# The first 23 microseconds of a fused spectral-mixing and GEGLU backward kernel, put in another order

## The chip, the cores and the metric

The kernel runs on one core of one Trainium2 chip. The metric is the device time in microseconds. Before the change it is 1395.79 us, the median of 4 runs that lie between 1395.49 and 1397.18. One more execution was taken with the hardware profiler on; all durations in this text come from it.

## The reference

The forward function gates two branches row by row. Branch A is a learned filter in the two-dimensional frequency domain, branch B a GEGLU feed-forward block. The kernel computes the output and the gradients with respect to everything but `B_x`, which branch B doesn't use: both branches read the same `x`.

```python
x = A_x                                              # 2048 x 576, bf16
g = sigmoid((x * gate_w).sum(-1, keepdims=True))
a = irfft2(rfft2(x) * (w_r + 1j * w_i))              # over rows and columns
b = (gelu(x @ w_gate) * (x @ w_up)) @ w_down         # F = 4608
out = g * a + (1 - g) * b
_out, vjp = jax.vjp(f, A_x, A_w_r, A_w_i, B_w_gate, B_w_up, B_w_down, gate_w)
grads = vjp(grad_out)                                # grad_out is dO below
```

## The kernel before

**Tiling.** The 2048 rows are 16 tiles of 128 rows; four of them form a row block, so there are four row blocks (`m`). The 4608 hidden columns are 18 groups (`g`) of 256. The outer loop runs over `g`, the inner one over `m`. For each pair the kernel computes `z = dO @ w_down.T` (lines 413 and 418), `xy = x @ [w_gate, w_up]` (lines 422 and 429), the gelu and its derivative on ScalarE and VectorE (lines 441 to 497), and stores the products for later. Between these, TensorE also does the weight gradients of the group before (lines 541, 559, 573) and pieces of the Fourier transforms (lines 602 to 875), which are written as products with sine and cosine tables. A last stage (line 1210) computes the gradient with respect to `x`.

**Layouts.** TensorE contracts over the partition axis, so `x` and `dO` are needed with their 576 columns on the partitions: `xT` and `dOT`, in five chunks of columns (four of 128 and a tail of 64). They are made by TensorE: a product with the identity matrix turns 128 x 128 elements into PSUM (`titems`, lines 378 to 384), and ScalarE or VectorE copies the result out (line 385). One call of `titems` gives three items, with chunks 0 and 1, chunks 2 and 3, and the tail; each item takes one PSUM buffer and one copy. The first group's `w_down` is turned in the same way into `wdT`; for the later groups a DMA transposes.

**PSUM.** While group 0 is computed there are four pools: `pg` with two buffers (transposes, and the small product of the gate), `ph` with two (`xy`, and some transposes as `fx`), and `pz` with one (`z`, and the warm-up). A transpose into `pg` waits until the copy out of the buffer that was used two turns before is done.

**The head.** The order of all work is written out by hand; no scheduler changes it. SyncE issues the loads in the order dO (tiles 0 to 3), `w_down` of group 0, `x` (tiles 0 to 3), the gate and up weights, and then the other tiles of dO and `x` in turn. A load waits for the completion of one about eight loads earlier, since the completion semaphores are reused. ScalarE's queue carries the one-row load of `gate_w` and the weights' tails. TensorE runs 30 products with the identity as warm-up (line 896), turns `gate_w` (line 901), and then turns dO and `w_down`. `H_mm(g, m, between)` computes `z` chunk by chunk and calls the functions in `between` before the tail chunk of `z`. For the first row block this is `opening`, which turns `x`, computes the sines, the parity tables and the first angles of the row transform, and calls `gate(0)`: 20 products with one column (line 394), a sigmoid (line 396), and two small operations that give `1 - g`, by which `z` is scaled (line 441).

**Tables.** `build_D` makes a cosine and a sine table for the transform over the 576 columns and is called for three sets (`D0`, `D2`, `D4`). Each gives functions for the angles (VectorE, lines 136 and 138), for the sines (ScalarE, lines 141 and 142), and for the tails (VectorE, line 152). `build_R` makes the angles of the transform over the rows (VectorE, lines 165 to 172); its sines come much later. ScalarE needs one function table for sines and another for sigmoids, and loads it when the first sigmoid comes.

Of the kernel before, what the change touches and what calls it, by code (L numbers as in the profile page):

```python
# [9 lines left out]
ACT = mybir.ActivationFunctionType  # L10
ALU = mybir.AluOpType
BF16 = mybir.dt.bfloat16
# [32 lines left out]
def eo(c):  # L45

    return slice(256 * (c % 2) + c // 2, 256 * (c % 2) + 256, 2)
# [208 lines left out]
def kernel(  # L256
# [4 lines left out]
    nc = tc.nc  # L261
    LD = nc.sync
# [6 lines left out]
    unit = Unit(ctx.enter_context(tc.tile_pool(name="unit", bufs=NUNIT, side="right")), "unit")  # L269
# [7 lines left out]
    do_v = grad_out[0].rearrange("(p t) d -> p t d", t=T)  # L277
# [19 lines left out]
    wts = {}  # L297
# [26 lines left out]
    def load_x(t0):  # L324
        LD.dma_start(xn[:, t0:t0 + 4, :], x_v[:, t0:t0 + 4, :])

    def load_do(t0):
        LD.dma_start(dB[:, t0:t0 + 4, :], do_v[:, t0:t0 + 4, :])

    ident = res.tile([P, P], BF16, name="ident")  # L330
    make_identity(nc, ident[:])
    gwr = unit([D], name="gwr")
    nc.scalar.dma_start(gwr[0:1, :], gate_w.rearrange("(o d) -> o d", o=1))
    load_do(0)
    wdn = unit([2, D], name="wdn")
    LD.dma_start(wdn[:], B_w_down[0:FG, :].rearrange("(c p) d -> p c d", p=P))
    load_x(0)
    load_w(0, 0, nc.scalar)
    for k in range(1, 4):
# [30 lines left out]
    def titems(src, dst, t0, ps, copies, n=4):  # L370
# [15 lines left out]
            return f  # L386
        return [item(k, cs) for k, cs in enumerate(((0, 1), (2, 3), (4,)))]

    def gate(k):
        lps = pgtile()  # L390
        ts = slice(4 * k, 4 * k + 4)
        for t in range(4 * k, 4 * k + 4):
            for ci in range(5):
                nc.tensor.matmul(lps[:, t:t + 1], lhsT=xT[:, ci, t, :], rhs=gwT[:, (ci, 4 + t % 2)[ci == 4]:][:, 0:1],
                                 start=(ci == 0), stop=(ci == 4))
        nc.scalar.activation(g_bf[:, ts], lps[:, ts], ACT.Sigmoid)
        nc.scalar.activation(omg_bf[:, ts], g_bf[:, ts], ACT.Identity, bias=1.0, scale=-1.0)
        nc.scalar.copy(omg32[:, ts], omg_bf[:, ts])
# [1 line left out]

    kept = {}

    def H_mm(g, m, between=()):

        wgu, wdT = wts[g]
        ts = range(4 * m, 4 * m + 4)
        z = pz.tile([P, 2, 2, FG], F32, tag="z", name="z")

        def zo(t):
            return z[:, t % 2, t % 4 // 2, :]  # L410
        for t in ts:
            for ci in range(4):
                nc.tensor.matmul(zo(t), lhsT=dOT[:, ci, t, :], rhs=wdT[:, ci, :], start=(t % 4 < 2 and ci == 0), stop=False)  # L413
        for f in between:
            f()
        for t in ts:
            r = (LO, HI)[t % 2]
            nc.tensor.matmul(zo(t), lhsT=dOT[r, 4, t, :], rhs=wdT[r, 4, :], start=False, stop=t % 4 >= 2)  # L418
        xy = [ph.tile([P, 2, 2 * FG], F32, tag="xy", name="xy") for _ in range(2)]
        for t in ts:  # L420
            r = (LO, HI)[t % 2]
            nc.tensor.matmul(xy[t % 4 // 2][:, t % 2, :], lhsT=xT[r, 4, t, :], rhs=wgu[r, 4, :], start=True, stop=False)  # L422

        def full(k, between=None):
            for t in ts[2 * k:2 * k + 2]:
                if t % 2 and between:
                    between()
                for ci in range(4):
                    nc.tensor.matmul(xy[k][:, t % 2, :], lhsT=xT[:, ci, t, :], rhs=wgu[:, ci, :], start=False, stop=(ci == 3))  # L429
            return xy[k]  # L430
        return z, full
# [469 lines left out]
        nc.tensor.matmul(gps[r, c:c + 1], lhsT=w, rhs=one[:], start=True, stop=True)  # L901
    D0 = build_D(nc, tb, unit, 0, 2)
    D0[0]()
    D0[1]()
    AC(gwT[:, 0:4], gps[:, 0:4])
    for c, r in ((4, LO), (5, HI)):
        AC(gwT[r, c:c + 1], gps[r, c:c + 1])
    D2 = build_D(nc, tb, unit, 2, 2)
    D2[0]()
    D4 = build_D(nc, tb, unit, 4, 1)  # L910
    parity = iotas_R(nc, tb, res, unit)
    for f in titems(dB, dOT, 0, (pgtile, pgtile, phtile), (VC, AC, VC)):
        f()
    for f in titems(wdn, wts[0][1][:].rearrange("p k (c m) -> p k c m", c=2), 0, (phtile, pgtile, phtile), (AC, VC, VC), n=2):
        f()
    makeB = build_B(nc, tb, unit, res)

    def opening():
        for f in titems(xn, xT, 0, (pgtile, pgtile, pgtile), (VC, AC, VC)):
            f()  # L920
        D2[1]()
        D4[0]()
        D4[1]()
        parity()
        D4[2]()
        build_R(nc, tb, unit, 0)
        gate(0)

    fg = zipped(*fwd_units(xT, scr_x, None)) + zipped(*fwd_units(dOT, scr_g, gs32))
    ia, pa = inv_units(scr_p1, a_dv, SD2)  # L930
# [61 lines left out]
    for g in range(NG):  # L992
# [3 lines left out]
        for m in range(NPR):  # L996
# [15 lines left out]
            if g == 0:  # L1012
                def items(src, dst, t, *cp):
                    return titems(src, dst, 4 * t, (pgtile,) * 3, cp) if t < NPR else [None] * 3
                do1 = items(dB, dOT, 1, VC, VC, VC) if m == 0 else []
                do2 = items(dB, dOT, m + 2, AC, AC, VC)
                x1 = items(xn, xT, m + 1, AC if m else VC, VC, VC)
                z, xy_full = H_mm(g, m, ([opening] if m == 0 else []) + rest)
                rest = []
                da = H_da(g, m, z)  # L1020
                if m == 0:
                    early, mid_, late_ = do1[:2], [do1[2], x1[0]], x1[1:]
                elif m < NPR - 1:
                    early, mid_, late_ = x1[:1], x1[1:], []
                else:
                    early, mid_, late_ = [], [], []
                for f in early:
                    f()
                xy = xy_full(0)
                for f in mid_:  # L1030
                    f()
                if held:
                    held.pop()()
                for part in (1, 0):
                    H_act(0, xy, tiles, part)

                def between():
                    for f in late_:
                        f()
                xy = xy_full(1, between)  # L1040
                for part in range(2):
                    H_act(1, xy, tiles, part)
                if m == 0:
                    build_R(nc, tb, unit, 4)
                    columns_B(nc, tb, res)
                elif m == 1:
                    next(makeB)
                if m < NPR - 1:
                    gate(m + 1)
                else:  # L1050
                    V.tensor_copy(g32[:], g_bf[:])
                    V.tensor_scalar(gs32[:], g32[:], SD2, None, op0=ALU.mult)
                if m + 2 < NPR:
                    do2[0]()
                    rest = do2[1:]
                state += [*H_ew1(g, tiles, da), da]
                held.append(sigs)
            else:
                z, xy_full = H_mm(g, m)
                da = H_da(g, m, z)  # L1060
                for f in inside:
                    f()
                if pr == 5:
                    scale_dB(2, AC)
                xy = xy_full(0)
                if held:
                    scale_dB(0, AC)
                    held.pop()()
                for part in (1, 0):
                    H_act(0, xy, tiles, part)  # L1070
                k0 = int(n > 0 and pr > 7 and ready())
                xy = xy_full(1, fft_next if k0 else None)
                for part in range(2):
                    H_act(1, xy, tiles, part)
                if pr == 5:
                    scale_dB(3, VC)
                state += [*H_ew1(g, tiles, da), da]
                if pr == 4:
                    scale_dB(1, VC)
                elif pr == 5:  # L1080
                    build_R(nc, tb, unit, 8)
                    build_R(nc, tb, unit, 12)
                elif pr == 6:
                    next(makeB)
                side_work(4.4)
                jobs = carry + hs
                total = sum(w for w, _ in jobs)
                at, k = 0.0, k0
                tables = {6: 0}.get(pr)
                for i, (w, f) in enumerate(jobs):  # L1090
                    if k < n and (at >= total * k / n - 0.45 or len(jobs) - i <= n - k):
                        fft_next()
                        k += 1
                    if i == tables:
                        run_late(tb)
                        wcopy[0] = VC
                    if pr == NG * NPR - 1 and at == 0.0:
                        sigs()
                    f()
                    at += w  # L1100
                wcopy[0] = AC
                while k < n:
                    fft_next()
                    k += 1
                flush()
                if pr == 6:
                    next(makeB)
                if pr < NG * NPR - 1:
                    sigs()
# [250 lines left out]
```

## Time and profile before

| what | value |
|---|---|
| median of 4 runs | 1395.79 us |
| the profiled execution | 1397.23 us |
| its span, from the first to the last instruction | 1395.5 us |
| TensorE busy | 1373.7 us, 98% of the span |
| VectorE, ScalarE, GpSimd busy | 740.1, 710.3, 245.4 us |
| granted TensorE clock, mean | 0.999 |
| second row block's `z` starts at | 22.94 us |

In a timeline each row gives the start in microseconds from the start of the span, the time from the start of the first instruction of the row to the end of its last, the engine, the line, the tile written and the tiles read, their shapes, and the number of instructions; idle time before the row and what ended it stand in brackets. PE is TensorE, DVE is VectorE, ACT is ScalarE, POOL is GpSimd and SP is SyncE. Matmuls overlap, so the sum of their durations is longer than the time they take, and a row's end is the end of its last one. In the windows, each engine has its busy time and, in brackets, its number of instructions, in the order PE, weight loads, DVE, ACT, POOL, and then the granted clock (1.00 is full), the busy share of the DMA engines and their rate.

### The profile page before, as it was taken

Reading aid. Unit: us, or ns where it says so; the run is one execution under the profiler, and the core shown is the slowest. Engines: PE = TensorE matmul, PEld = TensorE weight load, DVE = VectorE, ACT = ScalarE, POOL = GpSimd, SP = SyncE. Lnnn points to the kernel's source line nnn. Section 1 sums busy time; section 2 is a strip of 40 time slices with the busy share of each in tenths; the row PEclk is TensorE's granted clock in tenths of the full one; section 3 lists DMA queues with packets and bytes.
Section 4 is the critical chain, followed back from the end, with each engine's and each line's share of the span. In section 5 each row is a group of like instructions: output and inputs, shape, how many; then the busy total and the mean of one; then the engine's idle time right before and its main releaser. Section 6 shows DMA issues by size and latency. Waiting matters only on the chain.

```text
span 1395.5 us, 25930 instructions
## 1 busy us (share of the span) xinstructions
PE 1373.7 (98%) x10186; PEld 913.5 (65%) x10272; DVE 740.1 (53%) x1406; ACT 710.3 (51%) x1311; POOL 245.4 (18%) x486
## 2 busy tenths in 40 slices
PE   8999999999999999999999999999999999999999
PEld 6556566565566556556566566556777777777777
DVE  6975655555889777875666666560001742212101
ACT  6877767777778778767767777661000000000000
POOL 3000111123345634512111101110000100000000
PEclk9999999999999999999999999999999999999999
DMA  6433445355466556555556465749999997777774
GB/s 215 121 92 110 124 111 134 93 144 157 113 163 154 154 146 162 141 145 136 150 140 171 122 169 151 179 110 285 195 192 203 220 194 167 162 157 168 153 153 90
DMA packets 510647, 214.49 MB, mean 154 GB/s; under 512 B 312539, under 2 KB 503709, under 8 KB 510525
## 3 DMA queue, kind: packets, MB, share of 16 engines
q1 hardware_dynamic: 493402, 187.44, 57.2%
q0 software_dynamic: 14912, 24.24, 6.3%
q8 instruction: 80, 1.31, 0.4%
q10 hardware_dynamic: 2210, 1.15, 0.3%
q14 instruction: 43, 0.34, 0.1%
HBM read 41.05 MB, written 93.84 MB: 97 GB/s over the span
## 4 chain that ended last, share of the span: by engine, by line
PE 90%; ACT 2%; issue 1%; DMA 0%; SPq 0%; DVE 0%; ACTq 0%
PE acc L1210 30%; PE wps L559 16%; PE xy L429 15%; PE wps L541 9%; PE z L413 8%; PE wps L573 2%; PE xy L422 2%; PE pf L602 2%; PE z L418 1%; PE pf L619 1%; PE pf L873 1%; PE pf L800 1%; PE pf L711 1%; PE pf L875 1%; ACT ZT L850 0%
## 5 line engine op out<-in xcount | busy, mean ns | idle before, releaser
L1210 PEld LDWEIGHTS <-pin 128*128 128x128 bf16 x3456 | 337.7, 98 | 86.0 <-issue 0.3
L559 PE MATMUL wps<-dH,xn 128*128 128x512 bf16 x1135 | 270.0, 379 | 1.3 <-DVE dwd L510 0.5
L429 PE MATMUL xy<-wgu,xT 128*128 128x512 bf16 x1083 | 259.5, 381 | 8.5 <-issue 7.2
L429 PEld LDWEIGHTS <-xT 128*128 128x128 bf16 x1152 | 106.8, 98 | 134.0 <-issue 26.5
L559 PEld LDWEIGHTS <-xn 128*128 128x128 bf16 x1152 | 111.4, 98 | 118.7 <-issue 1.3
L1227 ACT COPY bo<-acc 128x288 f32<-128x288 f32 x32 | 12.7, 398 | 305.0 <-PE acc L1210 305.0
L541 PE MATMUL wps<-dB,A 128*128 128x288 bf16 x1152 | 154.2, 286 | 0.7 <-DVE dB L990 0.6
L566 POOL DMA_DIRECT2D out_dram<-dw x134 | 72.9, 547 | 432.3 <-ACT dw L510 390.7
L1210 PE MATMUL acc<-wgT,pin 128*128 128x288 bf16 x1152 | 143.8, 286 | 0.0
L1210 PE MATMUL acc<-wuT,pin 128*128 128x288 bf16 x1152 | 143.6, 286 | 0.0
L1210 PE MATMUL acc<-wd_all,pin 128*128 128x288 bf16 x1152 | 142.6, 286 | 0.0
L413 PE MATMUL z<-wdT,dOT 128*128 128x256 bf16 x1152 | 137.5, 273 | 1.3 <-ACT wdT L385 0.8
L541 PEld LDWEIGHTS <-A 128*128 128x128 bf16 x1152 | 112.0, 98 | 34.4 <-issue 1.3
L441 ACT ACTIVATE da<-z,omg 128x256 bf16<-128x256 f32 x288 | 112.1, 472 | 32.9 <-PE z L418 32.9
L413 PEld LDWEIGHTS <-dOT 128*128 128x128 bf16 x1152 | 112.4, 98 | 23.5 <-issue 2.5
L450 ACT CAST xb<-xy 128x512 bf16<-128x512 f32 x144 | 85.4, 593 | 49.9 <-PE xy L429 49.5
L1282 DVE SCALAR_TENSOR_TENSOR f32t<-gwf,dlog,b16t 128x576 f32<-128x576 f32 x16 | 13.1, 817 | 176.0 <-DMA b16t<-dxa_scr 176.0
L448 ACT ACTIVATE q<-xy 128x512 bf16<-128x512 f32 x144 | 88.1, 616 | 7.0 <-PE xy L429 5.0
L451 ACT CAST hu<-xy 128x512 bf16<-128x512 f32 x144 | 87.8, 610 | 0.0
L487 DVE TENSOR_TENSOR xb<-xb,sg 128x1024 bf16<-128x1024 bf16 x48 | 33.2, 691 | 96.5 <-ACT sg L479 96.5
L510 ACT CAST dw<-wps 128x512 bf16<-128x512 f32 x72 | 42.3, 589 | 54.6 <-PE wps L559 52.3
L456 DVE TENSOR_SCALAR s<-q 128x1024 bf16<-128x1024 bf16 x72 | 30.6, 425 | 69.9 <-ACT q L448 69.7
(220 smaller groups left out, 1635.5 us busy)
## 6 DMA issues: line engine op xcount, KB each, us to landing
scr<-dH SPq DMA_DIRECT2D x144, 256.0 KB, 3.4
scr<-A SPq DMA_DIRECT2D x72, 256.0 KB, 2.6
out_dram<-dw POOLq DMA_DIRECT2D x134, 64.0 KB, 2.5
wd_all<-in_B_w_down_dram SPq DMA_DIRECT2D x3, 1728.0 KB, 9.3
out_dram<-dwd POOLq DMA_DIRECT2D x34, 144.0 KB, 2.8
scr_p<-Vt SPq DMA_DIRECT2D x32, 145.0 KB, 3.0
wgu<-in_B_w_gate_dram SPq DMA_DIRECT2D x18, 256.0 KB, 4.2
wgu<-in_B_w_up_dram SPq DMA_DIRECT2D x18, 256.0 KB, 3.4
```

Of the source, the lines that this page charges most:

```text
L413: nc.tensor.matmul(zo(t), lhsT=dOT[:, ci, t, :], rhs=wdT[:, ci, :], start=(t % 4 < 2 and ci == 0), stop=False)
L429: nc.tensor.matmul(xy[k][:, t % 2, :], lhsT=xT[:, ci, t, :], rhs=wgu[:, ci, :], start=False, stop=(ci == 3))
L441: nc.scalar.activation(da[:, t, :], z[:, t % 2, t // 2, :], ACT.Copy, scale=omg32[:, 4 * m + t:4 * m + t + 1])
L448: nc.scalar.activation(q[:, h, :], xy[:, :, 0:FG], ACT.Square)
L450: nc.scalar.copy(xb[:, h, :], xy[:, :, 0:FG])
L451: nc.scalar.copy(hu[:, h, :], xy[:, :, FG:2 * FG])
L487: V.tensor_tensor(xb[:], xb[:], s[:], op=ALU.mult)
L510: wcopy[0](out, in_)
L541: nc.tensor.matmul(wps[:, :288], lhsT=tl(0, t)[:, fch * P:(fch + 1) * P], rhs=dB[:, t, h * 288:(h + 1) * 288], start=(t == 0), stop=(t == ...
L559: nc.tensor.matmul(wps[:].rearrange("p a b -> p (a b)"), lhsT=xn[:, t, c * P:(c + 1) * P], rhs=kt[t // 4][1][:, t % 4].rearrange("p k f -> ...
L566: wst[0].dma_start(ov[:, c, fsl], dw[:, k, :])
L1210: nc.tensor.matmul(acc[:, :288], lhsT=src[:, r, :], rhs=w_of(r)[:, h * 288:(h + 1) * 288], start=(first and r == 0), stop=(last and r == F ...
```

## The change

The change has five parts, all in the head.

1. SyncE loads `w_down` of group 0 before dO, and dO's first four tiles come in two loads of two tiles.
2. `w_down` is turned before dO. VectorE copies its first and last item and ScalarE the middle one. The sines of `D0` follow ScalarE's copy.
3. The first row block's dO is turned by pairs of tiles: `pair` puts all four full chunks of two tiles into one buffer, so that one copy (VectorE for the first pair, ScalarE for the second) completes two tiles. The tail of the four tiles is an item as before.
4. `x` is turned in the middle of `z`: `H_mm` has a new argument `amid`, called after the first two tiles of `z`. `opening` moves there; it turns the tail of `x` first, and VectorE makes all three copies. The gate stays where it was, before the tail of `z`. The first angles of the row transform move behind the first two transposes of the second row block's dO.
5. The sines of `D2` and `D4` are computed before `x` is turned, and after them ScalarE computes a sigmoid of one column that nobody reads, so that the table load comes there and not at the gate.

```diff
-    def load_do(t0):
-        LD.dma_start(dB[:, t0:t0 + 4, :], do_v[:, t0:t0 + 4, :])
+    def load_do(t0, n=4):
+        LD.dma_start(dB[:, t0:t0 + n, :], do_v[:, t0:t0 + n, :])
...
-    load_do(0)
     wdn = unit([2, D], name="wdn")
     LD.dma_start(wdn[:], B_w_down[0:FG, :].rearrange("(c p) d -> p c d", p=P))
+    load_do(0, 2)
+    load_do(2, 2)
     load_x(0)
...
+    def pair(src, dst, t0, ps, cp):
+
+        tp_ = ps(BF16).rearrange("p (c t m) -> p c t m", c=4, t=2)
+        for c in range(4):
+            for tt in range(2):
+                nc.tensor.transpose(tp_[:, c, tt, :], src[:, t0 + tt, eo(c)], ident[:])
+        cp(dst[:, 0:4, t0:t0 + 2, :], tp_)
+
...
-    def H_mm(g, m, between=()):
+    def H_mm(g, m, between=(), amid=None):
...
         for t in ts:
+            if amid and t == ts[2]:
+                amid()
             for ci in range(4):
...
     D0[0]()
-    D0[1]()
     AC(gwT[:, 0:4], gps[:, 0:4])
...
     D4 = build_D(nc, tb, unit, 4, 1)
+    for f in titems(wdn, wts[0][1][:].rearrange("p k (c m) -> p k c m", c=2), 0, (phtile, pgtile, phtile), (VC, AC, VC), n=2):
+        f()
+    D0[1]()
+    pair(dB, dOT, 0, pgtile, VC)
+    pair(dB, dOT, 2, pgtile, AC)
+    titems(dB, dOT, 0, (None, None, phtile), (None, None, VC))[2]()
+    D4[0]()
+    D2[1]()
+    D4[1]()
+    nc.scalar.activation(tb.warm[:], tb.halfpi[:], ACT.Sigmoid)
     parity = iotas_R(nc, tb, res, unit)
-    for f in titems(dB, dOT, 0, (pgtile, pgtile, phtile), (VC, AC, VC)):
-        f()
-    for f in titems(wdn, wts[0][1][:].rearrange("p k (c m) -> p k c m", c=2), 0, (phtile, pgtile, phtile), (AC, VC, VC), n=2):
-        f()
     makeB = build_B(nc, tb, unit, res)
 
     def opening():
-        for f in titems(xn, xT, 0, (pgtile, pgtile, pgtile), (VC, AC, VC)):
+        x0 = titems(xn, xT, 0, (pgtile, pgtile, phtile), (VC, VC, VC))
+        for f in (x0[2], x0[0], x0[1]):
             f()
-        D2[1]()
-        D4[0]()
-        D4[1]()
         parity()
         D4[2]()
-        build_R(nc, tb, unit, 0)
-        gate(0)
...
-                z, xy_full = H_mm(g, m, ([opening] if m == 0 else []) + rest)
+                z, xy_full = H_mm(g, m, [lambda: gate(0)] if m == 0 else rest, opening if m == 0 else None)
...
                 for f in early:
                     f()
+                if m == 0:
+                    build_R(nc, tb, unit, 0)
                 xy = xy_full(0)
```

## The prediction

> **What bounds the kernel now.** I read the page's engine shares first, then TensorE's timeline over the head, then the same stretch in windows (busy time and granted clock), and last ScalarE's and SyncE's timelines.
>
> ```profile
> PE 1373.7 (98%) x10186; PEld 913.5 (65%) x10272; DVE 740.1 (53%) x1406; ACT 710.3 (51%) x1311; POOL 245.4 (18%) x486
> ```
>
> TensorE is the bound over the whole span, and the change touches the first 23 us alone; what it can win is TensorE's idle or slow time there. Its timeline (start, duration, line, what waited):
>
> ```profile
> 5.18 1.07 PE L378 MATMUL pf<-ident,dB 128*128 128x128 bf16 x16
> 6.31 0.39 PE L378 MATMUL fx<-ident,wdn 128*128 128x128 bf16 x4
> 8.11 1.91 PE L413 MATMUL z<-wdT,dOT 128*128 128x256 bf16 x16 [0.82 <-ACT wdT L385]
> 9.86 1.06 PE L378 MATMUL pf<-ident,xn 128*128 128x128 bf16 x16
> 11.25 0.38 PE L384 MATMUL pf<-ident,xn 128*128 128x128 bf16 x4 [0.34 <-DVE xT L385]
> 12.01 0.69 PE L394 MATMUL pf<-gwT,xT 128*128 128x1 bf16 x20 [0.38 <-ACT xT L385]
> 14.98 0.94 PE L378 MATMUL pf<-ident,dB 128*128 128x128 bf16 x8 [0.96 <-ACT g_bf L396]
> 16.57 2.42 PE L429 MATMUL xy<-wgu,xT 128*128 128x512 bf16 x6 [0.22 <-issue]
> 22.94 1.91 PE L413 MATMUL z<-wdT,dOT 128*128 128x256 bf16 x16
> ```
>
> Four waits, 2.5 us by the brackets: on ScalarE's copy of w_down, on the copies of x (two), on the gate. And 16.57: six 512-column products take 2.42, where eight take 1.89 in the next row block (29.24). The windows say why (columns: window, length, busy by engine, clock, DMA share, GB/s):
>
> ```profile
> 8.10:11.60 3.50, 3.15 (x36) 2.76 (x36) 0.69 (x1) 0.65 (x1) 0.00 (x0) 1.00 1.08 360
> 11.60:15.00 3.40, 2.06 (x38) 1.43 (x37) 2.94 (x13) 3.26 (x8) 0.00 (x0) 1.00 1.00 398
> 15.00:18.40 3.40, 3.18 (x14) 1.72 (x15) 2.27 (x6) 1.93 (x6) 0.00 (x0) 0.51 1.02 386
> ```
>
> After a window with 2.06 of 3.40 busy the clock is halved for 3.4 us. ScalarE, which holds two of those waits:
>
> ```profile
> 6.56 1.01 ACT L385 COPY dOT<-pf 128x1024 bf16<-128x1024 bf16 x1
> 7.47 0.59 ACT L385 COPY wdT<-fx 128x512 bf16<-128x512 bf16 x1
> 13.46 1.28 ACT L396 ACT_TABLE_LOAD   x1
> 14.76 0.17 ACT L396 ACTIVATE g_bf<-pf 128x4 bf16<-128x4 f32 x1
> ```
>
> The table load stands in front of the gate's sigmoid, and the second transpose of the next dO waits for the PSUM buffer that this sigmoid reads.
>
> **What the Trainium skill says.** "TensorE: Matmul & The Clock Gate", Part 1: the clock falls to half after a window of about 3.4 us with too little activity, the window runs freely, and so the cold stretch varies between runs. The trace agrees (0.51 for 3.4 us). Part 4 there says that transposes do not count as activity; here the clock stays full after 4.81-8.10, which is nearly all transposes. "ScalarE: Activation LUTs", What ACT_TABLE_LOAD costs: 1283 ns and a drain of 1380; the trace has 1.28 and no drain after it (14.76). "DMA: Bandwidth & Descriptors", Queues, rings and completion order: one queue's descriptors start in ring order, which holds here: dO, w_down and x come in the order issued.
>
> **The change, part by part.** Arithmetic is the same: every transpose, copy and product is still there, one 1-column sigmoid (0.20) is added, and one load is split in two. I restart the head with durations from the rows above and from the same timelines: a 128-column transpose every 0.055 (20 in 5.18-6.3), readable 0.27 after its start (5.57 to 5.84); a z product 0.107; a 512-column product 0.214 (1.67/7 and 1.89/8 less the last one's latency); VectorE copies 0.69, 0.42, 0.28 for 1024, 512, 256 columns; ScalarE copies 1.01 and 0.59.
>
> Loads. SyncE's order becomes w_down (288 KB), two halves of dO (288 KB each), x. Before, dO's 576 KB were the first to land: SyncE's up-projection load, which waits for them, went out at 5.15, and the transposes at 5.18. The first 576 KB now are w_down and half of dO: w_down by 5.1, first half about 5.2-5.8, second at 6.0-6.5 (w_down before: 1.20 + 4.8 = 6.0). The split costs one more issue (0.42), so x is issued at about 2.2 instead of 1.67; the queue ahead of it is busy to 5, so it keeps its place, 1.67 + 6.4 = 8.1. It now waits for the one-row gate load, over by 2.20 when the old gate-weight load with the same wait went out. The gate-weight load now waits for w_down (about 5.1) rather than going at 2.20; the queue ahead (x) is busy to 7, so the transfer starts no later. Later loads wait for earlier ones in the same chain, byte for byte as before. Small tables fall on other buffers, and a few later instructions wait for the gate-row and w_down loads, landed by 6: nothing.
>
> w_down. Transposes at 5.18, 5.40, 5.62, done 5.84. VectorE is free at 5.89 (row 5.43 + 0.46, unchanged): two copies to 6.59. ScalarE: table 5.28, warm-up, three gate copies to 5.87, w_down copy to 6.46, D0 sines (0.86) to 7.3.
>
> dO. The pair copies write four runs of 256 instead of two of 512; no row shows that shape, so 0.69 (as the same columns take) to 1.1 (one column each 1.04 ns); I take 0.69, since the 256-column run in the w_down copy costs no more per column beyond its start. First pair 5.86-6.25, copied by VectorE 6.59-7.27; second pair waits for the w_down buffer (6.46): 6.51-6.9, copied by ScalarE 7.2-8.23; tail to 7.12, copied to 7.81.
>
> z and x. z of the first pair starts at 7.32 (before: 8.11, all of it) and ends 8.18. x tail 8.18-8.40, first half to 8.84, second to 9.28 (ScalarE's buffer free at 8.23). Second z 9.28-10.14, which hides VectorE's copies of x: D4's angles to 8.48, tail to 9.04, 9.74, 10.43. All three on VectorE cost 1.80; without the z between them TensorE would stand 1.1 us. The gate waits for the last, 10.48, ends 11.05.
>
> Sines and table. ScalarE: D2 and D4 sines (0.86 + 0.65) from 8.23 to 9.75, table to 11.04, warm sigmoid 11.24, gate sigmoid at 11.3. The wait of 0.96 is gone, because the table load now runs under x and z. Queued behind it are only g and the da copies, wanted once z ends at 11.28.
>
> Next. z tail and xy tail (0.23 + 0.52) end 11.80; dO of the second row block is needed here, 1.6 us sooner than before. By queue order 2.7 MB lie up to its end; the windows show 0.83 MB moved by 5.0 and 1.75 from 5 to 10, so it lands between 10.9 and 12.2: I charge 0.2. Transposes 12.0-12.88, xy to 14.6, transposes to 15.25. VectorE's R angles (1.14 + 0.43) now stand after these dO copies, at 14.04-15.65, and hold back the next dO and x copies: x buffers at 16.05 and 16.74, where TensorE arrives at 16.1 and 16.54: 0.25 lost. xy ends 17.86, gate and dO transposes 18.94. So the second row block's z starts at about 19.05, against 22.94.
>
> Sum: 22.94 - 19.05 = 3.9 us, of which 2.2 are waits and order and 1.7 the half-clock stretch (eight xy products 15.72-18.82, at full clock 1.71; 3.10 - 1.71 = 1.4, and 0.3 in the transposes before). VectorE and ScalarE move with it: by the same count VectorE's first-block work ends 4.1 sooner, so it does not take the gain back although it is 93% busy from 30 to 65 us. Later stages keep their order.
>
> The profiled execution took 1397.23 for a span of 1395.5: 1397.23 - 3.9 = 1393.3. Its own four timed neighbours run from 1395.49 to 1397.18, median 1395.79; the profiled one is 1.7 above the fastest, the size of one half-clock stretch. From a run without that stretch the gain is 2.2: 1395.49 - 2.2 = 1393.3. Both agree; I take 1393.1, since the 0.2 for dO's landing may not be due.
>
> **Rivals.**
> (1) Everything comes off the median: the 1.4 between profiled time and median is the cost of profiling, and the stretch sits in every run. 1395.79 - 3.9 = 1391.9. For it: the shortage of work at 11.6-15.0 is in the program. Against: two of four timed runs are at 1395.5 and one at 1397.18.
> (2) The half-clock stretch stays, or moves to the first transposes, since the window runs freely. 1393.1 + 1.7 = 1394.8. For: before 4.8 the 30 warm-up products take 3.38, 0.11 each, at half pace. Against: any 3.4 us after 5.2 now hold at least 2.6 of busy time.
> (3) Loads late: the first transfer ramps slowly (165 GB/s mean to 5.0, against 349 after), and w_down comes as 256 rows of 1152 bytes rather than 128 of 4608. If rows, not bytes, set the ramp, w_down is 0.5-1 late, and so is all behind it: 1394.0.
> (4) Slower: the same mechanism at its worst. w_down's wait takes the place of the ScalarE wait, and second-block dO comes late by more than the slack. It decides once w_down lands 2.2 us after 5.18, at 7.4; at 8.0 the time is 1396.1, with the half-clock stretch behind such a hole 1397.8, and past 1398.6 from 8.8 on. Against: w_down landed at 6.0 behind twice its bytes.
> That the change doesn't do what it says: the built order shows the moves, so only the wait could survive it.
>
> **Numbers.** A run cannot tell less than about 0.2% (2.8 us, so below 1393.0 is faster, above 1398.6 slower). Main case 0.58, 1392.2 to 1394.0, half of it under 1393.0; (1) 0.17; (2) 0.11; (3) 0.09; (4) 0.05, of which 0.03 beyond 1398.6. Faster: 0.29 + 0.17 = 0.46; slower 0.03; same 0.51. The range from 1391.6 to 1395.0 takes in (1), (2) and (3).
>
> **What would show it.** TensorE: w_down transposes at 5.2, z in two groups of 8, the first near 7.3, the second near 9.3; no wait on w_down's ScalarE copy; the dO transposes of the second row block without wait on g; second z group of 16 near 19.0; clock 1.00 from 15 to 18.4. ScalarE: table load near 9.8. Wrong if w_down's transposes start after 5.6, if xy of the first row block starts after 13.5, or if row block two gains 3.9 and the end does not.

## The result and the profile after

The changed kernel takes 1393.88 us (median of 42 runs, 1393.44 to 1395.92), the kernel before 1395.61 beside it (60 runs, 1395.46 to 1397.24). The ratio is 0.9987 with a 95% interval of 0.9982 to 0.9991: 1.7 us faster, and within the 0.2% that the prediction calls the same. The time lies in the predicted range (1391.6 to 1395.0), 0.8 above the predicted 1393.1. The profiled execution took 1393.88 for a span of 1392.00, against 1397.23 and 1395.45 before. Nine of the 60 runs of the kernel before lie between 1397.02 and 1397.24, and the execution profiled before is one of that kind: this matters below.

The page's engine shares, after:

```profile
PE 1371.9 (99%) x10186; PEld 913.3 (66%) x10272; DVE 740.7 (53%) x1407; ACT 710.0 (51%) x1311; POOL 244.7 (18%) x486
```

TensorE's timeline over the head, after (columns as in the prediction):

```profile
5.05 0.40 PE L379 MATMUL fx<-ident,wdn 128*128 128x128 bf16 x4
...
7.25 1.05 PE L424 MATMUL z<-wdT,dOT 128*128 128x256 bf16 x8
8.74 0.40 PE L385 MATMUL fx<-ident,xn 128*128 128x128 bf16 x4 [0.44 <-DMA xn<-in_A_x_dram]
...
9.87 1.04 PE L424 MATMUL z<-wdT,dOT 128*128 128x256 bf16 x8
...
12.26 1.07 PE L379 MATMUL pf<-ident,dB 128*128 128x128 bf16 x16
...
19.00 1.25 PE L424 MATMUL z<-wdT,dOT 128*128 128x256 bf16 x10
```

The four waits of before (0.82, 0.34, 0.38, 0.96) are gone. One new one stands there: 0.44 for the transfer of `x`. `w_down` is turned first and in time, `z` comes in two groups of eight, and the second row block's `z` starts at 19.00 instead of 22.94. Two of the stretches shown of before, in windows (length, busy by engine, clock, DMA share, GB/s):

```profile
11.60:15.00 3.40, 3.35 (x34) 2.01 (x33) 2.92 (x9) 2.14 (x7) 0.00 (x0) 1.00 1.03 411
15.00:18.40 3.40, 3.40 (x47) 2.42 (x45) 3.03 (x9) 1.82 (x4) 0.00 (x0) 1.00 1.04 390
```

The thin window (2.06 busy of 3.40) is full now (3.35), and the next one is at full clock. ScalarE's timeline, after:

```profile
9.31 1.28 ACT L930 ACT_TABLE_LOAD   x1
...
11.61 0.17 ACT L405 ACTIVATE g_bf<-pf 128x4 bf16<-128x4 f32 x1 [0.80 <-PE pf L403]
```

The table load runs under `x`'s transposes and the second group of `z`, and the gate's sigmoid now waits for TensorE instead of TensorE for it.

So the head gained what the prediction said, 3.94 us between the two profiles. The time gained less. Where the rest went is seen by following the gain through the program, with the starts of three events in both profiles:

| event | before | after | gain |
|---|---|---|---|
| second row block's `z` | 22.94 | 19.00 | 3.94 |
| last product of the kernel (its start) | 1392.14 | 1388.26 | 3.88 |
| end of the span | 1395.45 | 1392.00 | 3.45 |
| time of that execution | 1397.23 | 1393.88 | 3.35 |

Nothing is taken back in the 1370 us between the head and the last product (0.06). Behind the last product 0.43 is, and another 0.10 lies outside the span. And the execution profiled before is not the usual one, which the first experiment shows.

### The profile page after: what moved, and what is told of

It is laid out like the page before. It is cut to its first block, busy times and chain, and to the rows that moved or that the text cites. A ratio compares the mean times of both kernels' runs of the same rounds, so it can differ in the third digit from the quotient of the medians.

```text
span 1392.0 us, 25935 instructions
## 1 busy us (share of the span) xinstructions
PE 1371.9 (99%) x10186; PEld 913.3 (66%) x10272; DVE 740.7 (53%) x1407; ACT 710.0 (51%) x1311; POOL 244.7 (18%) x486
## 4 chain that ended last, share of the span: by engine, by line
PE 92%; ACT 3%; DVE 3%; issue 1%; DMA 1%; SPq 0%; DVEq 0%; ACTq 0%
PE acc L1224 30%; PE wps L570 16%; PE xy L440 16%; PE wps L552 10%; PE z L424 8%; PE wps L584 2%; PE xy L433 2%; PE pf L613 2%; PE z L429 2%; PE pf L630 1%; PE pf L884 1%; PE pf L811 1%; PE pf L722 1%; PE pf L886 1%; DMA xn<-in_A_x_dram 0%
```

## The experiments

My theory after the result: (a) the head gains 2.2 to 2.3 us in a usual execution, and the 1.7 of the half-clock stretch belong to some executions only; (b) the gain is carried whole to the last product; (c) 0.4 is lost after it, since one load more in the head shifts on which completion semaphore the last store ends; (d) within the head, the table load, `w_down` first and `x` in the middle of `z` each have a part. The rivals: the half-clock stretch sits in all executions, and something else eats 1.7; the table load alone makes the gain; the loads are late as in the prediction's rival (3). Each run's ratio is to the kernel before, run beside it on the same chip. Its medians there are 1395.61, 1395.79, 1395.93 and 1396.03, so times from different sets are compared by their ratios. The copies of `w_down` (part 2) and the pairs of tiles (part 3) were not run alone.

**The kernel before, profiled once more.** No edit.

> The kernel before, profiled once more, to see whether the half-clock stretch at 15 to 18.4 us belongs to the program or to one execution. Theory 1 (free-running window, the stretch is in few executions): clock 1.00 in 15.0-18.4, second row block's z at 21.2 to 21.4 us instead of 22.94, profiled time 1395.5. Rival (the stretch is in every execution): clock 0.5 again for 3.4 us, z at 22.9, and the profiled time near 1397.

Measured: 1395.61. TensorE's timeline of this execution:

```profile
14.98 0.61 PE L378 MATMUL pf<-ident,dB 128*128 128x128 bf16 x8 [0.97 <-ACT g_bf L396]
15.43 1.89 PE L429 MATMUL xy<-wgu,xT 128*128 128x512 bf16 x7
...
21.27 1.47 PE L413 MATMUL z<-wdT,dOT 128*128 128x256 bf16 x12
```

The waits are nearly the same (0.69, 0.34, 0.38 and 0.97), the thin window too (2.05 busy of 3.40 in 11.60 to 15.00), but the `xy` products at 15.43 run at full pace: eight up to 17.16, 0.216 each. The second row block's `z` starts at 21.27, 1.67 earlier than in the first profile, and the time is 1.62 lower. So the thin window costs 1.7 in some executions and nothing in others, and rival (1) of the prediction, which took 3.9 off the median, falls. From here the changed kernel is compared with this profile: 2.27 at the second row block's `z`, 2.23 at the last product (1390.49 to 1388.26), 1.80 at the end of the span (1393.80 to 1392.00), 1.73 in time.

Why one execution fell to half clock and the other did not can be read in part from the clock in the traces. In the first profile full clock begins at 4.85 and half clock at 15.09, which is 10.24 or three times 3.41 later, and half clock lasts 3.41. Counted in steps of 3.41 from where full clock begins, the step just ahead of half clock is 11.68 to 15.09. In the second profile full clock begins at 5.44, and the same step lies at 12.27 to 15.68. In windows, the first profile and then the second:

```profile
11.68:15.09 3.41, 2.11 (x38) 1.52 (x38) 3.02 (x14) 3.27 (x8) 0.00 (x0) 1.00 1.01 401
```

```profile
12.27:15.68 3.41, 2.44 (x41) 1.74 (x41) 2.99 (x14) 3.20 (x9) 0.00 (x0) 1.00 0.99 378
```

So the same waits left 2.11 busy in the one step and 2.44 in the other, because the steps lie elsewhere. That this decides is argued: only one profile here holds a half-clock stretch. The thinnest step that was followed by full clock held 2.29 (5.58 to 8.99 in the profile with one load less, below).

**The changed kernel once more.** No edit.

> The changed kernel, unaltered, beside the other three on one chip. Second z near 19.0 us; 3.7 us from the start of the last product to the end of the span, as in its first profile; 1393.9.

Measured: 1394.01 (21 runs, 1393.58 to 1396.00), ratio 0.9987 (0.9981 to 0.9994). Second `z` at 18.93, the wait for `x` 0.31, the end as in the first profile of it. The result repeats.

**Where the 0.4 at the end comes from.** SyncE's queue stores the last tile and then waits for it. SyncE at the end of the changed kernel, in the timeline:

```profile
1389.07 0.34 SPq L1302 DMA_DIRECT2D out_dram<-b16t  x1
```

and of the kernel before (second profile):

```profile
1391.29 0.34 SPq L1288 DMA_DIRECT2D out_dram<-b16t  x1
```

From the issue of this store to the end of the span: 1392.00 - 1389.07 = 2.93 after, 1393.80 - 1391.29 = 2.51 before. The store's own transfer is no slower: it lands 1.58 after its issue in both (1390.65 - 1389.07 after). The difference lies behind the landing. In the traces the transfers of SyncE and ScalarE come back on completion semaphores in turn, and at the end SyncE checks eight of them one after the other, always in the same order. The last store ends on the first of the eight in the changed kernel and on the last of them before, because the split of dO's load adds one transfer to the row. The checks as they stand in the traces, from the landing of the store to the last of the eight (ns shortest, median and longest, then the starts of the first and the last): changed kernel, 1390.66 to 1391.15,

```profile
L1369 SPq EVENT_SEMAPHORE  x8: 27/28/28, 1390.7 to 1391.1; - x8
```

and kernel before (second profile), 1392.88 to 1392.95:

```profile
L1355 SPq EVENT_SEMAPHORE  x1: 27/27/27, 1392.9 to 1392.9; - x1
```

In the changed kernel the first check waits for the store until 1390.67, and seven more follow, 0.06 apart; the next instruction of SyncE starts at 1391.16. Before, seven checks are through at 1392.1, while the store is still on its way, and only the eighth waits for it, until 1392.89; the next instruction starts at 1392.96. From the passing of the store's check to that next instruction it takes 0.49 after and 0.07 before: this is the 0.4. Two runs test it from both sides. First, the changed kernel with one load less (dO's row blocks 2 and 3 in one):

```diff
     for k in range(1, 4):
-        load_do(4 * k)
+        if k < 3:
+            load_do(4 * k, 4 * k)
         load_x(4 * k)
```

> The changed kernel with the loads of dO's third and fourth row blocks made one load, so that it has as many loads as the kernel before and the last store uses the same one of the eight completion semaphores as there (the last in the row, not the first). Theory 1 (the closing wait goes through the semaphores in a row, and the last store now sits on the first): second z unchanged at 19.0, but 3.3 us from the last product's start to the end instead of 3.7, and the time 0.4 us lower, 1393.5. Rival (the 0.4 us is the landing of the last store, which varies): 3.7 or any value, no steady gain.

Second, the kernel before with its first load of dO split:

```diff
-    def load_do(t0):
-        LD.dma_start(dB[:, t0:t0 + 4, :], do_v[:, t0:t0 + 4, :])
+    def load_do(t0, n=4):
+        LD.dma_start(dB[:, t0:t0 + n, :], do_v[:, t0:t0 + n, :])
...
-    load_do(0)
+    load_do(0, 2)
+    load_do(2, 2)
     wdn = unit([2, D], name="wdn")
```

> The kernel before with dO's first load split in two and nothing else. Theory 1 (the extra load costs at the end): head unchanged (second z at 21.3 without the half-clock stretch), 3.7 us from the last product to the end instead of 3.3, time 0.4 us above the kernel before (1395.9 to 1396.0). Rival (a split load costs nothing at the end): 1395.55.

Measured: one load less gives 1393.61 (21 runs, 1393.16 to 1395.62), ratio 0.9984 (0.9978 to 0.9991); the split gives 1396.47 (13 runs, 1395.80 to 1397.87), ratio 1.0004 (0.9996 to 1.0012). From the last product's start to the end of the span: 3.31 with one load less, 3.74 in the changed kernel, 3.73 with the split, 3.31 before. SyncE's waits at the end, changed kernel (engine, line, what for, total, times, longest):

```profile
SPq L1369 <- DMA out_dram<-b16t: 1.2, 1, 1.2
```

With one load less:

```profile
SPq L1370 <- DMA out_dram<-b16t: 0.7, 1, 0.7
```

All fourteen profiles agree. In seven (the changed kernel twice, the split, and four more below) SyncE and ScalarE together issue 857 transfers, the last store is on the first semaphore, and the wait is 1.2. In the other seven they issue 856, or 107 times eight, the store is on the last, and the wait is 0.7 or 0.8. So (c) is shown, from both sides and in the traces: here one transfer more in the row moves the end by 0.4. By its ratio the split costs about 0.6, more than 0.4, with an interval that also holds no change; its profile had the first transposes at half pace (16 of dO take 1.68 from 5.13 to 6.81, where the second profile of before takes 0.98), so its second `z` can't be compared.

The profile with one load less had a head of its own, which shows what the changed kernel is open to:

```profile
7.85 0.62 PE L396 MATMUL pf<-ident,dB 128*128 128x128 bf16 x8 [1.12 <-DMA dB<-in_grad_out_dram]
...
19.73 1.91 PE L425 MATMUL z<-wdT,dOT 128*128 128x256 bf16 x16
```

TensorE waited 1.12 for dO's second half. By the landings in the trace 15 of that transfer's 16 parts were in by 5.73 and the last at 7.81. "DMA: Bandwidth & Descriptors", section Why a DMA increments its semaphore by 16 and not by 1, of the Trainium skill says that up to 16 engines finish a transfer independently and only all 16 mean that it landed; here one of them was 2.1 us behind. Even so the time was 1394.15.

**The extra sigmoid.**

```diff
     D4[1]()
-    nc.scalar.activation(tb.warm[:], tb.halfpi[:], ACT.Sigmoid)
     parity = iotas_R(nc, tb, res, unit)
```

> The changed kernel without the one-column sigmoid that was put ahead. Theory 1 (the function table is loaded where the sigmoid stands, and that sigmoid waits for the gate's product): the load comes after the gate at 11.6 us, g at 12.9, the second dO transpose waits 0.4 us, second z at 19.4, about 0.4 us slower than the changed kernel. Rival (the load carries no wait and runs as soon as ScalarE is free): load still at 9.1 to 9.3 us, second z at 19.0, no difference.

Measured: 1394.10 (15 runs, 1393.56 to 1395.65), ratio 0.9985 (0.9977 to 0.9993); second `z` at 18.85. ScalarE's timeline:

```profile
9.68 1.28 ACT L405 ACT_TABLE_LOAD   x1
11.45 0.17 ACT L405 ACTIVATE g_bf<-pf 128x4 bf16<-128x4 f32 x1 [0.48 <-PE pf L403]
```

The load belongs to the gate's sigmoid (line 405) now, and still runs as soon as the last sine is issued, 1.8 before that sigmoid starts: it doesn't wait for the gate's products. The extra sigmoid is worth nothing. What counts is that no sines stand between it and the gate's products.

**Sines, table load and VectorE's copy of `x` alone.** The kernel before with these moves only: the angles of `D4`, the sines of `D2` and `D4` and the extra sigmoid ahead of the opening, and `x` copied by VectorE.

```diff
     D4 = build_D(nc, tb, unit, 4, 1)
     parity = iotas_R(nc, tb, res, unit)
...
+    D4[0]()
+    D2[1]()
+    D4[1]()
+    nc.scalar.activation(tb.warm[:], tb.halfpi[:], ACT.Sigmoid)
...
-        for f in titems(xn, xT, 0, (pgtile, pgtile, pgtile), (VC, AC, VC)):
+        for f in titems(xn, xT, 0, (pgtile, pgtile, pgtile), (VC, VC, VC)):
             f()
-        D2[1]()
-        D4[0]()
-        D4[1]()
```

> The kernel before, with one part of the change alone: x's copies all on VectorE, the angles of D4 and the sines of D2 and D4 with the one-column sigmoid ahead of the opening. The order of the loads, dO's pairs and the place of x stay as before. If the head's gain is the sum of its parts, the 0.96 us that the gate waited for the sigmoid's table goes, and the angles add 0.1 to 0.2: the second block's z starts at 20.3 to 20.5 (21.3 in the kernel before at full clock), the time is 0.8 to 1.0 lower than before: 1394.6 to 1394.8, ratio 0.9993 to 0.9995. If all parts were needed together (VectorE's copy of x comes after w_down and dO in the old order and the gate then waits for it), the time stays within 0.3 of 1395.6. The last store closes as in the kernel before (no load is added): from the last product's start to the end 3.3.

Measured: 1394.91 (13 runs, 1394.69 to 1395.32), ratio 0.9991 (0.9983 to 0.9999). TensorE's timeline:

```profile
13.40 1.07 PE L378 MATMUL pf<-ident,dB 128*128 128x128 bf16 x16
...
20.43 1.80 PE L413 MATMUL z<-wdT,dOT 128*128 128x256 bf16 x15
```

The 16 transposes of the second dO run in one piece where the kernel before waited 0.97 between the eighth and the ninth, and `z` comes at 20.43: 0.84 of the 2.27. This part gains without any of the others.

**`w_down` first.** The changed kernel with the old order of its loads, dO in one:

```diff
+    load_do(0, 4)
     wdn = unit([2, D], name="wdn")
     LD.dma_start(wdn[:], B_w_down[0:FG, :].rearrange("(c p) d -> p c d", p=P))
-    load_do(0, 2)
-    load_do(2, 2)
```

> The changed kernel with the old load order: dO whole, then w_down; the order of transposes stays new. Theory 1 (w_down first is a step on the path): w_down lands at 6.0 instead of before 5, its transposes start at 6.0 instead of 5.05, first z at 8.0 instead of 7.25, and 0.8 us is carried to the second z (19.8). Rival (x's landing is the bound at 8.7 us and swallows it): first z late by 0.8, the wait for x gone, second z at 19.2 to 19.3, time 0.2 to 0.3 us above the changed kernel.

Measured: 1394.87 (19 runs, 1393.64 to 1396.80), ratio 0.9988 (0.9981 to 0.9995). TensorE's timeline:

```profile
6.24 0.40 PE L378 MATMUL fx<-ident,wdn 128*128 128x128 bf16 x4 [1.05 <-DMA wdn<-in_B_w_down_dram]
...
8.43 1.05 PE L423 MATMUL z<-wdT,dOT 128*128 128x256 bf16 x8
...
19.57 1.91 PE L423 MATMUL z<-wdT,dOT 128*128 128x256 bf16 x16
```

Without the new order TensorE waits 1.05 for `w_down`, and `z` is 1.18 late (8.43 against 7.25). `x`, at 9.32, has landed by then, 0.89 after `z`'s start; in the changed kernel it follows 1.49 after it (7.25 to 8.74), so 0.60 is absorbed. What is left is 0.57 at the second `z`, and 0.43 of that comes back at the end (one load fewer: 3.31 there). In time the profiled execution is 0.2 above the changed kernel, but the runs fall into two groups, nine at 1393.64 to 1394.22 and ten at 1394.87 to 1396.80. The upper group was not profiled. All its runs list a mean clock of 1.000, where the execution of before with the half-clock stretch lists 0.999, so such a stretch does not fit; a late start of full clock, which the mean does not count (7.2 in the next profile, listed as 1.000), would, and the cause stays open.

**`x` after all of `z`.** The changed kernel, its opening where it was before:

```diff
-                z, xy_full = H_mm(g, m, [lambda: gate(0)] if m == 0 else rest, opening if m == 0 else None)
+                z, xy_full = H_mm(g, m, [opening, lambda: gate(0)] if m == 0 else rest, None)
```

> The changed kernel with x turned after all 16 products of z, copies still on VectorE. Theory 1 (the middle of z hides VectorE's copies): TensorE stands 1.1 us before the gate, but no longer waits 0.44 us for x to land; second z 0.2 to 0.4 us later (19.2 to 19.4), time 0.2 to 0.4 us above the changed kernel. Rival (x's landing is what counts, not where it is turned): second z at 19.0, no difference. Prediction's own figure, taken alone: 1.1 us later.

Measured: 1394.91 (13 runs, 1393.98 to 1397.07), ratio 0.9992 (0.9984 to 1.0000). TensorE's timeline:

```profile
8.18 1.92 PE L424 MATMUL z<-wdT,dOT 128*128 128x256 bf16 x16
...
11.56 0.20 PE L403 MATMUL pf<-gwT,xT 128*128 128x1 bf16 x2 [0.34 <-DVE xT L386]
12.16 0.60 PE L403 MATMUL pf<-gwT,xT 128*128 128x1 bf16 x18 [0.40 <-DVE par_i L107]
...
20.20 1.91 PE L424 MATMUL z<-wdT,dOT 128*128 128x256 bf16 x16
```

The gate waits twice for VectorE, 0.74 together, which the second group of `z` covers in the changed kernel. This execution came to full clock only at 7.2, so its `z` starts 0.93 later than in the other profile, and 20.20 against 19.00 overstates the edit. From the first `z` to the second row block's it takes 12.02; a variant below, in which TensorE also waits for no transfer, takes 11.14 with `x` in the middle. So the place is worth 0.88 where `x` is there in time. In the changed kernel's own profile (11.75) the lateness of `x` takes 0.6 of that back. By the ratios (0.9992 against 0.9987) the edit costs 0.7, with intervals that overlap.

**`x` copied by ScalarE again.**

```diff
-        x0 = titems(xn, xT, 0, (pgtile, pgtile, phtile), (VC, VC, VC))
+        x0 = titems(xn, xT, 0, (pgtile, pgtile, phtile), (VC, AC, VC))
```

> The changed kernel, x's copy in the opening given back to ScalarE, nothing else. ScalarE has the sines and the table load ahead of it until about 10.6, so a copy of about 1 us ends at 11.6 and the gate's product waits for it: 0.5 to 1.0 later at the second block's z (19.5 to 20.0), time 1394.4 to 1394.9. If ScalarE reaches the copy before its table load (the order of the stream decides), it ends by 10 and the time stays at 1393.9, within 0.3.

Measured: 1395.80 (13 runs, 1394.43 to 1397.37), ratio 0.9996 (0.9988 to 1.0004). ScalarE's timeline:

```profile
9.22 1.28 ACT L930 ACT_TABLE_LOAD   x1
...
10.62 0.99 ACT L386 COPY xT<-pf 128x1024 bf16<-128x1024 bf16 x1
```

TensorE's:

```profile
11.67 0.60 PE L403 MATMUL pf<-gwT,xT 128*128 128x1 bf16 x18 [0.79 <-ACT xT L386]
...
19.71 0.49 PE L424 MATMUL z<-wdT,dOT 128*128 128x256 bf16 x3
```

The copy stands behind sines and table load in ScalarE's order, and the gate waits 0.79 for it: 0.71 at the second `z`, 0.60 in the time of this execution (1394.48). Five of the 13 runs lie at 1394.43 to 1394.56, the other eight at 1395.72 and above; those were not profiled. Five of the eight (1396.54 to 1397.37) list a mean clock of 0.999, as the execution of before with the half-clock stretch does; the three at 1395.72 to 1395.81 list 1.000 and are not explained. The early table load and VectorE's copies thus belong together: without the copies 0.71 is lost. The table load without them was not run in the kernel before.

**The angles of the row transform at their old place.**

```diff
         parity()
         D4[2]()
+        build_R(nc, tb, unit, 0)
...
-                if m == 0:
-                    build_R(nc, tb, unit, 0)
```

> The changed kernel with the angles of R back at the end of the opening, ahead of dO's copies, nothing else. The prediction charged their new place with 0.25 us on the way to the first g. If that was right, the second block's z comes at 18.75 and the time is 1393.6 to 1393.8; if VectorE's place is covered by the gate's products either way, it stays within 0.15 of the changed kernel (1393.9). If the old place delays dO's copies, and dO's products stand for it, 0.2 to 0.3 later: 1394.1 to 1394.2.

Measured: 1394.13 (21 runs, 1393.72 to 1394.38), ratio 0.9987 (0.9980 to 0.9993). VectorE's timeline:

```profile
12.67 1.14 DVE L165 SCALAR_TENSOR_TENSOR XR<-kk,scol 128x128 int32<-128x128 f32 x4
...
14.19 1.73 DVE L386 COPY dOT<-pf 128x1024 bf16<-128x1024 bf16 x3
```

At the old place the copies of the second dO come at 14.19 instead of 12.91, and `x`'s transposes follow 2.18 after the first `xy` product (13.34 to 15.52) instead of 1.95 (13.16 to 15.11): 0.23 lost. The new place costs nothing: the changed kernel's timeline has no wait from 12.26 to 19.00. The prediction had charged it 0.25. (Its second `z` at 19.41 also holds a wait of 0.53 for dO's second half, so only the stretch from `xy` on is compared: 6.07 against 5.84.)

**The transfers on the path.** Two more kernels build on the one with one load less. In the first the four small tail loads of the weights go through SyncE behind `x` instead of ScalarE's queue:

```diff
-    load_w(0, 0, nc.scalar)
+    load_w(0, 0)
```

> As e6, and the four small loads of the gate and up weights' tail rows go out from SyncE behind x instead of from ScalarE ahead of it. Theory 1 (x's landing at 8.6 to 8.7 us is the last wait on the head's path, and 128 KB of small rows go ahead of it): x lands at 8.0 to 8.3, TensorE does not wait for it, second z at 18.5, time 0.4 us below e6 (1393.1). Rival (x is late because one of the 16 rings is slow, whatever goes ahead): x at 8.6, second z at 19.0, same time as e6.

In the second, `load_w` is written out in place, the tails go ahead of the main loads of the gate and up weights, and dO of the second row block is issued between the two (only this part is shown):

```diff
     for w, c0 in gu:
         for r in (LO, HI):
             LD.dma_start(wts[0][0][r, 4, c0:c0 + FG], w[512:D, 0:FG])
+    load_do(4)
     for w, c0 in gu:
         LD.dma_start(wts[0][0][:, 0:4, c0:c0 + FG].rearrange("p (e k) f -> p e k f", e=2),
                      w[0:512, 0:FG].rearrange("(k p e) f -> p e k f", e=2, p=P))
```

> The changed kernel with the merged load of dO's later rows (one load less), the weights' tails issued by SyncE behind x, and dO of the second block issued ahead of the main loads of gate and up. If the wait for x's transfer (0.3 to 0.4 in the changed kernel) and then the one for dO's second block (0.2 in the run with the tails behind x) are what is left of the loads on the path, both go: second block's z at 18.5 to 18.6, time 1393.2 to 1393.4, ratio 0.9982 to 0.9984. If the transfers share one limit and the gate's weights now land late, the wait moves to the gate and the time is 1393.7 or more.

Measured: 1393.71 (20 runs, 1393.01 to 1394.78), ratio 0.9984 (0.9977 to 0.9990), and 1393.57 (17 runs, 1392.99 to 1395.02), ratio 0.9982 (0.9975 to 0.9989). TensorE's timeline of the first:

```profile
12.08 1.07 PE L380 MATMUL pf<-ident,dB 128*128 128x128 bf16 x16 [0.20 <-DMA dB<-in_grad_out_dram]
```

and of the second:

```profile
18.85 1.36 PE L433 MATMUL z<-wdT,dOT 128*128 128x256 bf16 x11
```

In the first, `x` is turned from 8.30 on with no wait shown, dO of the second row block is 0.2 late in its place, and the second `z` starts at 18.84. In the second no transfer is waited for; its first `z` started at 7.71, 0.46 later than in the changed kernel (half pace up to 6.0), and by the second `z` that is made up. But the ratios don't tell these two from the kernel with one load less (0.9984). For the last the expected ratio was met (0.9982) and the expected time was not: the kernel before took 1396.03 beside it. The order with one load less, in any of the three, is the fastest found: ratios of 0.9982 to 0.9984 against 0.9987, with intervals that overlap.

## Why the prediction was right, and where it was not

**Restarting the head from durations held.** The transposes of `w_down` start at 5.05 (predicted 5.18), the first `z` at 7.25 (7.32), the table load at 9.31 (9.75), the gate's products end about 11.5 (11.05), the second row block's `z` at 19.00 (19.05). The pair copies, left open between 0.69 and 1.1 on VectorE, took 0.69, and 1.01 on ScalarE, as any copy of 1024 columns. Full clock from 15 to 18.4 came as said. `w_down` landed at 3.70 and dO's halves at 4.49 and 5.76, all earlier than charged (5.1, 5.2 to 5.8, 6.0 to 6.5), so the warm-up ahead of them and not `w_down` sets where the transposes start. One reading of the lines was wrong: by the brackets ScalarE holds three of the four waits of before, not two.

**Steps inside it were wrong and cancelled.** For `x`, "it keeps its place, 1.67 + 6.4 = 8.1" failed: it landed at 8.69, and its transposes started at 8.74 instead of 8.18, 0.56 late. The figure is right for the kernel before, where `x` landed at 8.02 and 8.20 in the two profiles; with dO loaded whole in two variants (sines alone, `w_down` second) it came at 8.14 and 8.25. With the split, it came at 8.53 in the kernel before with nothing else changed, and at 8.40 to 8.87 in the changed kernel and the variants with its order and number of loads (9.41 in the profile with one load less, whose dO was late as well). By these profiles it is the split that moves `x`; the prediction counted one more issue for it (0.42) and no delay of `x`. The four small loads on ScalarE's queue go out in both kernels and don't explain the difference, but taking them out of the way makes up for it (8.25 and 8.13). The first part of `x` lands no later than before (6.60 against 6.96), its last does; what holds it is not shown. Against that, two charges were not due: 0.25 for the row transform's angles, which cost nothing at their new place, and 0.2 for the second dO, which was not waited for at 12.26. It landed at 11.73, inside the stated range, though the prediction's own figures (2.7 MB, of which 0.83 and 1.75 had moved by 10) would put it at about 10.3. 0.56 less 0.45 is 0.1, and small differences in the copies make up that. That the sum met 19.05 to a tenth is luck as far as these steps go.

**"Without the z between them TensorE would stand 1.1 us"** measured 0.74 in waits and 0.88 from `z` to `z`, about the size said. **The wait of 0.96 "is gone, because the table load now runs under x and z"** is right on the cause; the moves of that part alone brought 0.84. The extra sigmoid had no part in it.

**The half-clock stretch.** That 1.7 belong to single executions, and that a run without them gains 2.2, was shown by the second profile of before (2.27). The prediction reasoned from two timed runs at 1395.5; 60 runs bear it out. The Trainium skill, "TensorE: Matmul & The Clock Gate", Part 1, says that the window runs freely and the point of change varies with it; the runs agree, and vary by more than the half microsecond it gives: full clock begins between 4.2 and 7.2 in the thirteen profiles here that list it.

**The step that failed is the last: the gain carried whole to the end.** By the profiles, 1397.23 - 3.94 = 1393.29; 0.06 was lost on the way to the last product, 0.43 behind it and 0.10 outside the span: 1393.88. From the second profile of before: 1395.61 - 2.27 + 0.04 + 0.43 + 0.07 = 1393.88 as well. The prediction named the semaphores that loads share and followed them through the head, and stopped there: it counted the split as "one more issue (0.42)" and didn't ask on which semaphore the last store would then close. That is the whole 0.4, shown from both sides. Its own sign of being wrong, "if row block two gains 3.9 and the end does not", came true for this part: of the 3.94, 3.45 arrived at the end of the span. The further 0.2 was taken off 1393.3 "since the 0.2 for dO's landing may not be due"; it was not due, but the lateness of `x` took its place.

**The rivals.** (1) fell, by the second profile of before. (2) did not occur in any profile of the changed kernel; two of its 42 runs lie 2 us above the median, and they alone of the 42 list a mean clock of 0.999, so they are likely of that kind, against nine of 60 before. (3) names 1394.0, closer than my own figure, but not for its reason: `w_down` and dO's halves came in time, and `x` cost 0.44. (4) did not occur; its trigger was `w_down` landing at 7.4, and it landed at 3.70. What is left of it is the risk seen in two profiles, one part of dO's second half about 2 us late, with waits of 1.12 and 0.53. Of the chance of 0.46 for a gain beyond 0.2%, 0.29 stood for the half of the main case under 1393.0. The 0.4 at the end alone does not account for its failing: without it the median would be about 1393.5, and the kernels that avoid it take 1393.57 to 1393.71.

## What to carry to other kernels

When a kernel that is bound by one engine has a thin start, restart that stretch instruction by instruction from the measured durations. Here the sum came out to a tenth although single steps were off by half a microsecond, because these happened to cancel, so check the steps and not the sum alone. Before subtracting a gain from a profile's time, profile the same kernel a second time: here 1.7 of 3.9 belonged to one execution. And when loads are added or removed anywhere, look at the end too, since the turn of the completion semaphores shifts for everything behind them.

## What was not expected of the hardware

- The end of the program takes 3.3 or 3.7 us from the last product's start, by the semaphore on which the last store completes (last or first of eight), since the checks of the others come behind it or while it is on its way.
- A table load runs 1.8 us ahead of its sigmoid while that waits for TensorE.
- One of a transfer's 16 parts can land 1.7 to 2.1 us after the other fifteen (dO's second half: 5.55 and 7.21 in one profile, 5.73 and 7.81 in another).
- The same thin stretch of the kernel before (2.06 and 2.05 busy of 3.40) was followed by half clock in one execution and by full clock in another; in steps of 3.41 us from where full clock began, it held 2.11 and 2.44.
- Splitting one load in two let another, two loads behind, land 0.3 to 0.5 us later (`x` in the kernel before: 8.02 and 8.20, with the split 8.53).
